# Packed attention and two feed-forwards on one core: a new instruction order for the second feed-forward

## The chip, the cores and the metric

The kernel runs on one core of a Trainium2 chip. The time is the device time of one execution in microseconds (us); a run of a kernel is one such execution, and the number compared is the median of several. The core has TensorE (PE in the rows, with its weight loads PEld), VectorE (DVE), ScalarE (ACT), GpSimd (POOL) and SyncE (SP), which issues the DMAs here. Each engine takes its instructions in the order in which the program lists them and waits on semaphores of the others.

## What is computed

Attention through 32 packed rows per head, then a gated feed-forward with RMS norm (width 512 to 1536), then a second feed-forward. Only the second one changes:

```python
def _moe2_ref(x, w_in, w_out):          # x: 4608 x 512, w_in: 512 x 2048, w_out: 2048 x 512
    h = x @ w_in
    g = h * np.cos(h)
    return (g @ w_out).astype(np.float32)
```

## The kernel before

All matrix products are made in three passes: each operand is split into a high and a low part (`hilo`, lines 110 to 112: a ScalarE copy, then a VectorE subtraction), and `mm3` (lines 154 to 157) multiplies high by high, high by low and low by high.

The second feed-forward is the loop from line 1107. The tokens come in nine chunks of 512 (`NCH`), the 2048 hidden columns in eight pairs of blocks of 128 (`NP2`); so there are 72 pairs `q`, and `p` is the pair before. For a pair, h is made by seven products of half-size blocks in place of eight (`prod(q, z, ...)`, six matmuls of 256 columns each), whose sums and differences are put together on VectorE and ScalarE: product 1 goes to PSUM tile `hx`, 2 to `hy`, 7 to `hz`, 6 adds to `hx`, 5 again to `hx`, 4 to `hz`, 3 to `hx`. Between them ScalarE copies intermediate states out: `p1` (line 1118, after product 1), `p7` (line 1128, after 7) and `u2` (line 1129, after 6); a later product on the same tile must wait until that copy has read it. VectorE adds `p1` (line 1121), `p7` (line 1144, into the second half of `hx`) and `u2` (line 1145). So h of a pair consists of two blocks, `s` = 0 (tile `h`, complete after product 4) and `s` = 1 (tile `hx`, complete after product 3 and line 1144).

For each block, g = h cos(h) is a chain of nine steps over 512 columns: `kk_a` (ScalarE, line 1026), `kk_b`, `r_a`, `r_b` (VectorE, 1030, 1034, 1040), `r_abs` and `r_sin` (ScalarE, 1044, 1048), `r_mul` (VectorE, 1052), `g_hi` (ScalarE, 1056) and `g_lo` (VectorE, 1060). In the trace the tiles are `kk`, `r` and `ghl`. Then `o_part` multiplies four token tiles of 128 by the block of the output weights (`w2hl`, split by `w2_split`), twelve matmuls of 512 columns for each block, into four PSUM tiles `ops` that collect all 16 blocks of a chunk. When a chunk is complete, `o_out` copies each tile to `ob` (ScalarE for even, VectorE for odd tiles, lines 1086 and 1084) and stores it (line 1098).

In the loop the second product of the pair two back, `o_part([(q - 2, 1)])`, stands in two stretches of two token tiles on either side of products 5 and 4, and `o_part([(q - 1, 0)])` behind product 3. While a chunk runs, the x of the next one is loaded and split on ScalarE and VectorE in pairs 2 to 7 of the chunk (`X_AT2`, `split_x`); `w_fetch(q + 3)` brings the first product's weights from DRAM, three buffers in all. The whole program has a fixed order (`tc.manual_schedule()`): every engine runs its instructions in the order of the code.

Of the kernel before, what the change touches and what calls it, by code (L numbers as in the profile page):

```python
# [9 lines left out]
F32 = mybir.dt.float32  # L10
F32R = mybir.dt.float32r
# [9 lines left out]
def kernel(  # L21
# [14 lines left out]
    nc = tc.nc  # L36
# [51 lines left out]
    X_AT = {11: (0,), 12: (1,), 13: (2,), 14: (3,), 15: (4,), 17: (5,), 19: (6,), 21: (7,)}  # L88
    X_AT2 = {2: (0,), 3: (1,), 4: (2,), 5: (3,), 6: (4, 5), 7: (6, 7)}
# [762 lines left out]
    def split_x(n, step):  # L852
        r0, r1 = x_r[n]
        lo, hi = slice(0, HT), slice(HT, TOK)
        a11, a21, a12, a22 = r0[:, :, lo], r0[:, :, hi], r1[:, :, lo], r1[:, :, hi]
        sub = lambda o, i0, i1: nc.vector.tensor_tensor(out=o, in0=i0, in1=i1, op=ALU.subtract)
        if step == 0:
            pool, tag = (late["b2"], "xs") if n else (pp_p, "pp0")
            x_s[0] = pool.tile([128, 2, HT], F32, tag=tag, name="xs", bufs=1)
            nc.vector.tensor_tensor(out=x_s[0], in0=a21, in1=a22, op=ALU.add)  # L860
            sub(a21, a11, a21)
            return
        src = (None, a11, a12, a21, a11, x_s[0], a12, a22)[step]
# [34 lines left out]
    def w2_load(f):  # L898
        assert ("o", f, 0) in w2_done
        pool, tag = late["w2"], ("raw", "ny")[f % 2]  # L900
        t = w2_r[f] = pool.tile([128, DM], F32, tag=tag, name="w2raw", bufs=2 + 2 * (f % 2))
        nc.sync.dma_start(out=t, in_=w2o_dram[f])
# [91 lines left out]
    for f in range(NF1):  # L994
        for d2 in range(2):
            acc_block(B, f, d2)
        if f + len(S_AT) < NF1:
            load_s(f + len(S_AT))
        w2_split(f)
        if f == NF1 // 2:  # L1000
            nc.scalar.activation(out=warm, in_=halfpi, func=AF.Sin)
        if f + 2 < NF1:
            w2_load(f + 2)
# [58 lines left out]
    def o_part(jobs, ts):  # L1062
        jobs = [j for j in jobs if j[0] >= 0]
        for t in ts:
            sl = slice(t * 128, (t + 1) * 128)
            for q, s in jobs:
# [6 lines left out]
                if k == NF2 - 1:  # L1073
                    o_out(n, t)
# [26 lines left out]
    def after(f, q, s):  # L1101
        if q >= 0:
            f(q, s)

    w_fetch(2)
    T = list(range(TOK // 128))
    for q in range(NQ + 1):
        p, on = q - 1, q < NQ
        n, fp = divmod(q, NP2)
        if on:  # L1110
            x = ps_h.tile([128, 2, HT], F32, tag="hx", name="hx", bufs=2)
            y, z = (ps_h.tile([128, 2, HT], F32, tag=t, name=t)[:, 0] for t in ("hy", "hz"))
            prod(q, 1, x[:, 0], True)
        after(r_mul, p, 0)
        after(r_abs, p, 1)
        if on:
            p1, p7, u2 = (b2.tile([128, HT], F32, tag=t, name=t, bufs=1) for t in ("p1", "p7", "u2"))
            nc.scalar.activation(out=p1, in_=x[:, 0], func=AF.Copy)
            prod(q, 2, y, True, True)
            h0 = b2.tile([128, 2, HT], F32, tag="h", name="h")  # L1120
            nc.vector.tensor_tensor(out=h0[:, 0], in0=y, in1=p1, op=ALU.add)
            prod(q, 7, z, True)
            prod(q, 6, x[:, 0], False)
        after(r_sin, p, 1)
        after(g_hi, p, 0)
        after(r_mul, p, 1)
        if on:
            nc.scalar.activation(out=p7, in_=z, func=AF.Copy)
            nc.scalar.activation(out=u2, in_=x[:, 0], func=AF.Copy)
        after(g_hi, p, 1)  # L1130
        after(g_lo, p, 0)
        if on:
            if n + 1 < NCH:
                if fp == 1:
                    load_x(n + 1)
                for step in X_AT2.get(fp, ()):
                    split_x(n + 1, step)
        after(g_lo, p, 1)
        if on:
            o_part([(q - 2, 1)], T[:2])  # L1140
            prod(q, 5, x[:, 0], False)
            prod(q, 4, z, False, True)
            o_part([(q - 2, 1)], T[2:])
            nc.vector.tensor_tensor(out=x[:, 1], in0=x[:, 0], in1=p7, op=ALU.add)
            nc.vector.tensor_tensor(out=h0[:, 1], in0=z, in1=u2, op=ALU.add)  # L1145
            h_t[q] = {"h": (h0.rearrange("p t n -> p (t n)"), x.rearrange("p t n -> p (t n)"))}
            kk_a(q, 0)
            kk_b(q, 0)
            r_a(q, 0)
            r_b(q, 0)  # L1150
            prod(q, 3, x[:, 0], False, True)
            w_fetch(q + 3)
            kk_a(q, 1)
            kk_b(q, 1)
            o_part([(q - 1, 0)], T)
            r_abs(q, 0)
            r_sin(q, 0)
            r_a(q, 1)
            r_b(q, 1)
        else:  # L1160
            o_part([(q - 2, 1)], T)
            o_part([(q - 1, 0), (q - 1, 1)], T)
# [30 lines left out]
```

## Time and profile before

| | us |
|---|---|
| median of three runs | 1658.41 |
| lowest and highest | 1651.59, 1667.56 |
| the profiled execution | 1651.87 |
| its span, first to last instruction | 1650.1 |
| TensorE busy | 1590.3 |
| VectorE, ScalarE busy | 1131.8, 897.1 |

The profiled execution is one of its own, beside the three. In it the second feed-forward's first product starts at 860.42 us and its last matmul at 1645.08 us. A matmul's busy time in the rows is longer than the distance between two starts, since matmuls overlap: 0.28 us for 256 columns at a distance of 0.12, 0.39 for 512 columns.

### The profile page before, as it was taken

The numbers are of one execution on the slowest core, as the hardware profiler recorded it, in microseconds if no ns is written. First come the engines' busy times: TensorE is split into PE (matmuls) and PEld (weight loads), VectorE is DVE, ScalarE is ACT, GpSimd is POOL, SyncE is SP. The second block draws the span as 40 slices with busy tenths as digits, with TensorE's granted clock in tenths as the row PEclk, the third lists the DMA queues.
The fourth block names the chain that finished last, engine by engine and source line by source line (L and its number), as shares of the span: only waits on it lengthen the run. The fifth ranks groups of instructions, "written<-read, shape, count | busy, mean of one in ns | idle before, by whom it ended". The sixth has DMA issues, their size and how long they took to land.

```text
span 1650.1 us, 29157 instructions
## 1 busy us (share of the span) xinstructions
PE 1590.3 (96%) x11216; PEld 1344.8 (82%) x11216; DVE 1131.8 (69%) x2203; ACT 897.1 (54%) x1796; POOL 32.8 (2%) x49
## 2 busy tenths in 40 slices
PE   7868999999999999999999999999999999999998
PEld 5536778888888787878988888888888888888887
DVE  4678866666666756665527777777777777777775
ACT  5556554455545454444426656565556565565654
POOL 1000110000000000000000000000000000000000
PEclk9989999999999999999999999999999999999999
DMA  9997644565555555556376454646454645454551
GB/s 265 310 257 236 200 149 148 168 190 165 184 186 172 178 182 180 196 163 207 104 276 227 179 209 165 220 179 230 169 201 174 228 179 214 171 209 179 183 200 26
DMA packets 129387, 315.97 MB, mean 191 GB/s; under 512 B 41696, under 2 KB 60128, under 8 KB 120032
## 3 DMA queue, kind: packets, MB, share of 16 engines
q1 hardware_dynamic: 129248, 314.10, 57.1%
q8 instruction: 89, 1.46, 0.4%
q14 instruction: 50, 0.41, 0.1%
HBM read 262.15 MB, written 51.90 MB: 190 GB/s over the span
## 4 chain that ended last, share of the span: by engine, by line
PE 87%; DMA 6%; DVE 3%; issue 1%; ACT 1%; POOL 0%; SPq 0%; DVEq 0%; POOLq 0%; ACTq 0%
PE ops L155 8%; PE ops L156 8%; PE ops L157 8%; PE gv L155 6%; PE acc L155 6%; PE gv L156 6%; PE gv L157 6%; PE acc L157 6%; PE acc L156 6%; PE hx L155 5%; PE hx L157 4%; PE hx L156 4%; PE mps L568 3%; DMA wo<-in_moe_w_gate_dram 2%; PE hz L155 2%; PE hz L156 2%
## 5 line engine op out<-in xcount | busy, mean ns | idle before, releaser
L155 PE MATMUL gv<-apt,wmhl 128*128 128x288 f32 x768 | 234.4, 305 | 1.7 <-ACT apt L111 0.9
L156 PE MATMUL gv<-apt,wmhl 128*128 128x288 f32 x768 | 228.3, 297 | 0.4 <-DVE apt L112 0.4
L156 PE MATMUL ops<-w2hl,ghl 128*128 128x512 f32 x576 | 227.1, 394 | 0.0
L155 PE MATMUL ops<-w2hl,ghl 128*128 128x512 f32 x576 | 227.0, 394 | 0.0
L157 PE MATMUL gv<-apt,wmhl 128*128 128x288 f32 x768 | 226.9, 295 | 0.0
L157 PE MATMUL ops<-w2hl,ghl 128*128 128x512 f32 x576 | 224.8, 390 | 0.0
L788 ACT ACTIVATE shl<-silu 128x288 fp32r<-128x288 f32 x192 | 85.4, 445 | 198.8 <-DVE silu L781 192.8
L155 PEld LDWEIGHTS gv<-apt,wmhl 128*128 128x128 f32 x768 | 145.4, 189 | 48.3 <-issue 17.3
L155 PE MATMUL acc<-shl,wohl 128*128 128x512 f32 x432 | 175.7, 407 | 1.2 <-ACT wohl L531 0.9
L157 PE MATMUL acc<-shl,wohl 128*128 128x512 f32 x432 | 170.2, 394 | 2.8 <-POOL wohl L534 2.7
L156 PE MATMUL acc<-shl,wohl 128*128 128x512 f32 x432 | 169.6, 393 | 0.0
L781 DVE TENSOR_TENSOR silu<-silu,gv 128x288 f32<-128x288 f32 x192 | 86.4, 450 | 99.9 <-PE gv L157 68.4
L156 PEld LDWEIGHTS gv<-apt,wmhl 128*128 128x128 f32 x768 | 145.2, 189 | 5.9 <-DVE apt L112 0.6
L157 PEld LDWEIGHTS gv<-apt,wmhl 128*128 128x128 f32 x768 | 145.2, 189 | 0.0
L1044 ACT ACTIVATE r<-r 128x512 f32<-128x512 f32 x144 | 91.1, 633 | 98.5 <-DVE r L1040 98.5
L1026 ACT ACTIVATE kk<-h,magic 128x512 f32<-128x512 f32 x72 | 52.1, 724 | 159.4 <-DVE h L1145 159.4
L157 PEld LDWEIGHTS ops<-w2hl,ghl 128*128 128x128 f32 x576 | 108.5, 188 | 24.7 <-DVE ghl L1060 0.5
L155 PEld LDWEIGHTS ops<-w2hl,ghl 128*128 128x128 f32 x576 | 109.1, 189 | 16.3
L156 PEld LDWEIGHTS ops<-w2hl,ghl 128*128 128x128 f32 x576 | 109.2, 190 | 14.9
L780 ACT ACTIVATE silu<-gv 128x288 f32<-128x288 f32 x192 | 78.4, 408 | 59.5 <-PE gv L157 58.7
L112 DVE TENSOR_TENSOR wmhl<-mps,wmhl 128x512 fp32r<-128x512 f32 x96 | 61.8, 685 | 70.5 <-ACT wmhl L111 70.5
L1060 DVE TENSOR_TENSOR ghl<-r,ghl 128x512 fp32r<-128x512 f32 x144 | 98.8, 686 | 11.9 <-ACT ghl L1056 11.8
(162 smaller groups left out, 3700.3 us busy)
## 6 DMA issues: line engine op xcount, KB each, us to landing
wa<-wa SPq DMA_DIRECT2D x72, 1024.0 KB, 4.9
wb<-wb SPq DMA_DIRECT2D x72, 768.0 KB, 6.5
wy<-wy SPq DMA_DIRECT2D x96, 512.0 KB, 4.6
kn<-in_k_dram SPq DMA_DIRECT2D x16, 576.0 KB, 9.5
vn<-in_v_dram SPq DMA_DIRECT2D x16, 576.0 KB, 9.2
qnat<-in_q_dram SPq DMA_DIRECT2D x32, 288.0 KB, 4.0
x_dram<-x SPq DMA_DIRECT2D x18, 512.0 KB, 3.1
x1raw<-x_dram SPq DMA_DIRECT2D x18, 512.0 KB, 8.1
```

The lines of the kernel that those rows point to most:

```text
L112: (eng or nc.vector).tensor_tensor(out=lo, in0=src, in1=hi.bitcast(F32), op=ALU.subtract)
L155: nc.tensor.matmul(ps, lhi, rhi, start=first, stop=False, skip_group_check=chain)
L156: nc.tensor.matmul(ps, lhi, rlo, start=False, stop=False, skip_group_check=chain)
L157: nc.tensor.matmul(ps, llo, rhi, start=False, stop=last, skip_group_check=chain)
L568: nc.tensor.matmul(ps[kt][h * NP:(h + 1) * NP], ppT[b // 4][rows, 4 * kt + h, n:n + NP], w_y[2 * u + kt][rows, j], start=True, stop=True,)
L780: nc.scalar.activation(out=t, in_=pss[0], func=AF.Silu)
L781: nc.vector.tensor_tensor(out=t, in0=t, in1=pss[1], op=ALU.mult)
L788: nc.scalar.activation(out=sh[:, 0, cols], in_=t, func=AF.Copy)
L1026: nc.scalar.activation(out=kk, in_=h, func=AF.Identity, scale=1.0 / TWO_PI, bias=magic[:, 0:1])
L1044: nc.scalar.activation(out=r, in_=r, func=AF.Abs)
L1060: nc.vector.tensor_tensor(out=g[:, 1], in0=h_t[q]["r", s], in1=g[:, 0].bitcast(F32), op=ALU.subtract)
```

## The change

Product 3 of a pair, which completes block `s` = 1, moves behind product 6 of the next pair (`p3`), and with it `kk_a`, `kk_b`, `r_a` and `r_b` of that block. The product of the pair two back stands in one stretch behind it, ahead of products 5 and 4; the other one ends the pair. The outputs of a chunk are no longer copied where they are complete, but collected (`outs`) and put at four places of the ScalarE and VectorE order (`o_evict`). `split_x` is divided into single steps: the high parts `h0` to `h6` and the sums `s1` to `s4`; `X_AT2` gives each pair two places, for ScalarE on either side of `p1` (`x_hi`), for VectorE behind `g_lo` of the pair before and between `kk_a` and `kk_b` (`x_lo`). The weights are fetched two pairs ahead, behind product 3 of the pair before. The splits of the output weights 10 and 11 move from the end of the first feed-forward into pairs 1 and 2, and their raw blocks lie in the two `pp` buffers. After the last pair the rest is written out, with one block's product after the other.

```diff
@@ -85,8 +85,10 @@
     AL_AT, CL_AT = 16, 21
     ATT_FROM, ATT_TO, ATT_FROM0, ATT_TO0, N_ATT = 0, 48, 10, 45, 32
     BX, BW = 9, 12
-    X_AT = {11: (0,), 12: (1,), 13: (2,), 14: (3,), 15: (4,), 17: (5,), 19: (6,), 21: (7,)}
-    X_AT2 = {2: (0,), 3: (1,), 4: (2,), 5: (3,), 6: (4, 5), 7: (6, 7)}
+    X_AT = {
+        11: ("s1", "s3"), 12: ("h0",), 13: ("h1", "s2"), 14: ("h2", "s4"), 15: ("h3",), 17: ("h4",), 19: ("h5",), 21: ("h6",)
+    }
+    X_AT2 = {2: ("s1", "s3"), 3: ("h0", "h1"), 4: ("s2", "h2"), 5: ("s4", "h3"), 6: ("h4", None), 7: ("h5", "h6")}
 
     wide = w_gate.dtype != F32
 
@@ -849,25 +851,31 @@
 
     x_r = {}
 
-    def split_x(n, step):
+    def split_x(n, step, part=None):
         r0, r1 = x_r[n]
         lo, hi = slice(0, HT), slice(HT, TOK)
         a11, a21, a12, a22 = r0[:, :, lo], r0[:, :, hi], r1[:, :, lo], r1[:, :, hi]
         sub = lambda o, i0, i1: nc.vector.tensor_tensor(out=o, in0=i0, in1=i1, op=ALU.subtract)
-        if step == 0:
-            pool, tag = (late["b2"], "xs") if n else (pp_p, "pp0")
-            x_s[0] = pool.tile([128, 2, HT], F32, tag=tag, name="xs", bufs=1)
-            nc.vector.tensor_tensor(out=x_s[0], in0=a21, in1=a22, op=ALU.add)
-            sub(a21, a11, a21)
+        if step[0] == "s":
+            if step == "s1":
+                pool, tag = (late["b2"], "xs") if n else (pp_p, "pp0")
+                x_s[0] = pool.tile([128, 2, HT], F32, tag=tag, name="xs", bufs=1)
+                nc.vector.tensor_tensor(out=x_s[0], in0=a21, in1=a22, op=ALU.add)
+            elif step == "s3":
+                sub(a21, a11, a21)
+            elif step == "s2":
+                sub(a11, x_s[0], a11)
+            else:
+                sub(a12, a12, a11)
             return
-        src = (None, a11, a12, a21, a11, x_s[0], a12, a22)[step]
-        t = wm_p.tile([128, 2, 2, HT], F32R, tag="wm", name="xhl")
-        x_t[n].append(t)
-        hilo(src, t[:, 0], t[:, 1])
-        if step == 2:
-            sub(a11, x_s[0], a11)
-        if step == 3:
-            sub(a12, a12, a11)
+        x = int(step[1])
+        src = (a11, a12, a21, a11, x_s[0], a12, a22)[x]
+        if part != 1:
+            x_t[n].append(wm_p.tile([128, 2, 2, HT], F32R, tag="wm", name="xhl"))
+            nc.scalar.activation(out=x_t[n][x][:, 0], in_=src, func=AF.Copy)
+        if part != 0:
+            t = x_t[n][x]
...
@@ -897,8 +905,11 @@
 
     def w2_load(f):
         assert ("o", f, 0) in w2_done
-        pool, tag = late["w2"], ("raw", "ny")[f % 2]
-        t = w2_r[f] = pool.tile([128, DM], F32, tag=tag, name="w2raw", bufs=2 + 2 * (f % 2))
+        if f in (NF1 - 2, NF1 - 1):
+            t = w2_r[f] = pp_p.tile([128, DM], F32, tag=f"pp{f % 2}", name="w2raw", bufs=1)
+        else:
+            tag = ("raw", "ny")[f % 2]
+            t = w2_r[f] = late["w2"].tile([128, DM], F32, tag=tag, name="w2raw", bufs=2 + 2 * (f % 2))
         nc.sync.dma_start(out=t, in_=w2o_dram[f])
...
@@ -996,7 +1007,8 @@
             acc_block(B, f, d2)
         if f + len(S_AT) < NF1:
             load_s(f + len(S_AT))
-        w2_split(f)
+        if f < NF1 - 2:
+            w2_split(f)
...
-    def o_part(jobs, ts):
+    def o_part(jobs, ts, outs=None):
...
@@ -1071,7 +1083,10 @@
                 k = o_n[n, t] = o_n.get((n, t), -1) + 1
                 mm3(o_t[n][t], g[:, 0, sl], g[:, 1, sl], w[:, 0], w[:, 1], k == 0, k == NF2 - 1)
                 if k == NF2 - 1:
-                    o_out(n, t)
+                    if outs is None:
+                        o_out(n, t)
+                    else:
+                        outs.append((n, t))
...
@@ -1102,64 +1117,102 @@
         if q >= 0:
             f(q, s)
 
+    def after(q, f, *a):
+        if q >= 0:
+            f(q, *a)
+
+    def x_hi(n, fp, slot):
+        if n + 1 < NCH and fp in X_AT2:
+            step = X_AT2[fp][slot]
+            if step is not None and step[0] == "h":
+                split_x(n + 1, step, 0)
+
+    def x_lo(n, fp, slot):
+        if n + 1 < NCH and fp in X_AT2:
+            step = X_AT2[fp][slot]
+            if step is not None:
+                split_x(n + 1, step, 1)
+
+    def o_evict(outs, n):
+        for x in outs[:n]:
+            o_out(*x)
+        del outs[:n]
+
     w_fetch(2)
     T = list(range(TOK // 128))
-    for q in range(NQ + 1):
-        p, on = q - 1, q < NQ
-        n, fp = divmod(q, NP2)
-        if on:
-            x = ps_h.tile([128, 2, HT], F32, tag="hx", name="hx", bufs=2)
-            y, z = (ps_h.tile([128, 2, HT], F32, tag=t, name=t)[:, 0] for t in ("hy", "hz"))
-            prod(q, 1, x[:, 0], True)
-        after(r_mul, p, 0)
-        after(r_abs, p, 1)
-        if on:
-            p1, p7, u2 = (b2.tile([128, HT], F32, tag=t, name=t, bufs=1) for t in ("p1", "p7", "u2"))
-            nc.scalar.activation(out=p1, in_=x[:, 0], func=AF.Copy)
-            prod(q, 2, y, True, True)
-            h0 = b2.tile([128, 2, HT], F32, tag="h", name="h")
-            nc.vector.tensor_tensor(out=h0[:, 0], in0=y, in1=p1, op=ALU.add)
-            prod(q, 7, z, True)
-            prod(q, 6, x[:, 0], False)
-        after(r_sin, p, 1)
-        after(g_hi, p, 0)
-        after(r_mul, p, 1)
-        if on:
-            nc.scalar.activation(out=p7, in_=z, func=AF.Copy)
-            nc.scalar.activation(out=u2, in_=x[:, 0], func=AF.Copy)
-        after(g_hi, p, 1)
-        after(g_lo, p, 0)
-        if on:
-            if n + 1 < NCH:
-                if fp == 1:
-                    load_x(n + 1)
-                for step in X_AT2.get(fp, ()):
-                    split_x(n + 1, step)
-        after(g_lo, p, 1)
-        if on:
-            o_part([(q - 2, 1)], T[:2])
-            prod(q, 5, x[:, 0], False)
-            prod(q, 4, z, False, True)
-            o_part([(q - 2, 1)], T[2:])
-            nc.vector.tensor_tensor(out=x[:, 1], in0=x[:, 0], in1=p7, op=ALU.add)
-            nc.vector.tensor_tensor(out=h0[:, 1], in0=z, in1=u2, op=ALU.add)
-            h_t[q] = {"h": (h0.rearrange("p t n -> p (t n)"), x.rearrange("p t n -> p (t n)"))}
-            kk_a(q, 0)
-            kk_b(q, 0)
-            r_a(q, 0)
-            r_b(q, 0)
-            prod(q, 3, x[:, 0], False, True)
-            w_fetch(q + 3)
-            kk_a(q, 1)
-            kk_b(q, 1)
-            o_part([(q - 1, 0)], T)
-            r_abs(q, 0)
-            r_sin(q, 0)
-            r_a(q, 1)
-            r_b(q, 1)
-        else:
-            o_part([(q - 2, 1)], T)
-            o_part([(q - 1, 0), (q - 1, 1)], T)
+    p3 = lambda q: prod(q, 3, h_t[q]["x"][:, 0], False, True)
+    for q in range(NQ):
+        p, n, fp = q - 1, q // NP2, q % NP2
+        if fp == 1 and n + 1 < NCH:
+            load_x(n + 1)
+        x = ps_h.tile([128, 2, HT], F32, tag="hx", name="hx", bufs=2)
+        y, z = (ps_h.tile([128, 2, HT], F32, tag=t, name=t)[:, 0] for t in ("hy", "hz"))
+        p1, p7, u2 = (b2.tile([128, HT], F32, tag=t, name=t, bufs=1) for t in ("p1", "p7", "u2"))
+        h0 = b2.tile([128, 2, HT], F32, tag="h", name="h")
+        h_t[q] = {"x": x, "h": (h0.rearrange("p t n -> p (t n)"), x.rearrange("p t n -> p (t n)"))}
+        prod(q, 1, x[:, 0], True)
+        prod(q, 2, y, True, True)
+        x_hi(n, fp, 0)
+        nc.scalar.activation(out=p1, in_=x[:, 0], func=AF.Copy)
+        nc.vector.tensor_tensor(out=h0[:, 0], in0=y, in1=p1, op=ALU.add)
+        x_hi(n, fp, 1)
+        after(p, r_abs, 0)
+        after(p, r_sin, 0)
+        prod(q, 7, z, True)
+        prod(q, 6, x[:, 0], False)
+        after(p, p3)
+        w_fetch(q + 2 if q else NCH * NP2)
+        outs = []
+        o_part([(q - 2, 1)], T, outs)
+        after(p, r_mul, 0)
+        after(p, kk_a, 1)
+        after(p, kk_b, 1)
+        after(p, r_a, 1)
+        after(p, r_b, 1)
+        after(p, g_hi, 0)
+        o_evict(outs, 2)
+        nc.scalar.activation(out=p7, in_=z, func=AF.Copy)
+        nc.scalar.activation(out=u2, in_=x[:, 0], func=AF.Copy)
+        o_evict(outs, 1)
+        after(p, g_lo, 0)
+        o_evict(outs, 1)
+        after(p, r_abs, 1)
+        after(p, r_sin, 1)
+        x_lo(n, fp, 0)
+        after(p, r_mul, 1)
+        after(p, g_hi, 1)
+        if q in (1, 2):
+            w2_split(NF1 - 3 + q)
+        prod(q, 5, x[:, 0], False)
+        prod(q, 4, z, False, True)
+        nc.vector.tensor_tensor(out=h0[:, 1], in0=z, in1=u2, op=ALU.add)
+        nc.vector.tensor_tensor(out=x[:, 1], in0=x[:, 0], in1=p7, op=ALU.add)
+        kk_a(q, 0)
+        x_lo(n, fp, 1)
+        kk_b(q, 0)
+        r_a(q, 0)
+        r_b(q, 0)
+        after(p, g_lo, 1)
+        o_part([(q - 1, 0)], T)
+    q = NQ - 1
+    p3(q)
+    o_part([(q - 1, 1)], T)
+    kk_a(q, 1)
+    r_abs(q, 0)
+    kk_b(q, 1)
+    r_a(q, 1)
+    r_b(q, 1)
+    r_sin(q, 0)
+    r_abs(q, 1)
+    r_mul(q, 0)
+    r_sin(q, 1)
+    g_hi(q, 0)
+    r_mul(q, 1)
+    g_lo(q, 0)
+    g_hi(q, 1)
+    g_lo(q, 1)
+    o_part([(q, 0)], T)
+    o_part([(q, 1)], T)
 
 
 # ---- launch: one core; inputs and outputs as the reference has them ----
```

ScalarE in a pair without splits or outputs, before. The names with numbers are tiles: `hx_10901` is this pair's `hx`, `r_10868` and `r_10898` are the two blocks of the pair before, `r_10975` is this pair's first block.

```order
L1118 ACTIVATE p1_10912<-hx_10901 128x256
L1048 ACTIVATE r_10898<-r_10898,halfpi_62 128x512
L1056 ACTIVATE ghl_10937<-r_10868 128x512
L1128 ACTIVATE p7_10913<-hz_10903 128x256
L1129 ACTIVATE u2_10914<-hx_10901 128x256
L1056 ACTIVATE ghl_10942<-r_10898 128x512
L1026 ACTIVATE kk_10972<-h_10922,magic_63 128x512
L1026 ACTIVATE kk_10988<-hx_10901,magic_63 128x512
L1044 ACTIVATE r_10975<-r_10975 128x512
L1048 ACTIVATE r_10975<-r_10975,halfpi_62 128x512
L1044 ACTIVATE r_11005<-r_11005 128x512
```

The same place with the change; here `hx_10883` is this pair's `hx` and `hx_10770` that of the pair before, `r_10867` and `r_10944` are the blocks of the pair before.

```order
L1156 ACTIVATE p1_10886<-hx_10883 128x256
L1056 ACTIVATE r_10867<-r_10867 128x512
L1060 ACTIVATE r_10867<-r_10867,halfpi_62 128x512
L1038 ACTIVATE kk_10941<-hx_10770,magic_63 128x512
L1068 ACTIVATE ghl_10947<-r_10867 128x512
L1174 ACTIVATE p7_10887<-hz_10885 128x256
L1175 ACTIVATE u2_10888<-hx_10883 128x256
L1056 ACTIVATE r_10944<-r_10944 128x512
L1060 ACTIVATE r_10944<-r_10944,halfpi_62 128x512
L1068 ACTIVATE ghl_10955<-r_10944 128x512
L1038 ACTIVATE kk_10971<-h_10889,magic_63 128x512
```

`kk` of the second block (`kk<-hx`) has moved from behind the first one's to the next pair, ahead of both copies `p7` and `u2`, and the first `ghl` with it; abs and sin of the second block now stand behind `u2`.

VectorE in the pair after a chunk's end, where the outputs are copied, before; `hx_10901` is `hx` of the pair before, `hx_11008` and `h_11029` are this pair's.

```order
L1052 TENSOR_TENSOR r_10975<-r_10975,h_10922 128x512
L1121 TENSOR_TENSOR h_11029<-hy_11009,p1_11019 128x256
L1052 TENSOR_TENSOR r_11005<-r_11005,hx_10901 128x512
L1060 TENSOR_TENSOR ghl_11044<-r_10975,ghl_11044 128x512
L1060 TENSOR_TENSOR ghl_11049<-r_11005,ghl_11049 128x512
L1084 COPY ob_11060<-ops_10213 128x512
L1084 COPY ob_11085<-ops_10215 128x512
L1144 TENSOR_TENSOR hx_11008<-hx_11008,p7_11020 128x256
L1145 TENSOR_TENSOR h_11029<-hz_11010,u2_11021 128x256
```

And with the change; `hx_10883` is `hx` of the pair before, `hx_10994` and `h_11000` are this pair's.

```order
L1157 TENSOR_TENSOR h_11000<-hy_10995,p1_10997 128x256
L1064 TENSOR_TENSOR r_10974<-r_10974,h_10889 128x512
L1042 TENSOR_SCALAR kk_11052<-kk_11052 128x512
L1046 SCALAR_TENSOR_TENSOR r_11055<-kk_11052,hx_10883 128x512
L1052 SCALAR_TENSOR_TENSOR r_11055<-kk_11052,r_11055 128x512
L1099 COPY ob_11060<-ops_10197 128x512
L1072 TENSOR_TENSOR ghl_11058<-r_10974,ghl_11058 128x512
L1099 COPY ob_11069<-ops_10199 128x512
L1064 TENSOR_TENSOR r_11055<-r_11055,hx_10883 128x512
L1188 TENSOR_TENSOR h_11000<-hz_10996,u2_10999 128x256
L1189 TENSOR_TENSOR hx_10994<-hx_10994,p7_10998 128x256
```

The two output copies stood directly ahead of the adds of `p7` and `u2`; now they stand on either side of the first `ghl` step, with the second block's multiplication between them and the adds, and the add of `u2` comes ahead of that of `p7`.

## Rows read from the trace of the kernel before

**Rows 1.** The page, busy us, share and instructions.

```profile
PE 1590.3 (96%) x11216; PEld 1344.8 (82%) x11216; DVE 1131.8 (69%) x2203; ACT 897.1 (54%) x1796; POOL 32.8 (2%) x49
```

**Rows 2.** Stretches between first hy products: us, busy (xinstructions) by engine, clock, DMA share, GB/s.

```profile
902.87:913.41 10.54, 10.54 (x68) 9.54 (x67) 7.73 (x15) 6.29 (x12) 0.00 (x0) 1.00 0.48 180
...
924.03:934.81 10.78, 10.78 (x68) 9.50 (x67) 8.41 (x16) 6.90 (x14) 0.00 (x0) 1.00 0.46 168
...
sum 76.04, PE 74.92 PEld 66.61 DVE 57.70 ACT 45.52 POOL 0.00; mean PE 10.70 PEld 9.52 DVE 8.24 ACT 6.50 POOL 0.00
...
881.79:1627.12 745.33, 736.34 (x4557) 656.96 (x4556) 560.71 (x1002) 446.92 (x832) 0.00 (x0) 1.00 0.52 188
```

**Rows 3.** Waits of PE from 860 us: total, times, longest.

```profile
PE hx L155 <- DVE hx L1144: 9.0, 8, 1.1
PE hx L155 <- ACT p L1118: 3.0, 1, 3.0
PE hx L155 <- ACT u L1129: 1.2, 2, 0.7
```

**Rows 4.** Timeline at an output pair, start and length first.

```profile
962.42 0.39 PE L157 MATMUL ops<-w2hl,ghl 128*128 128x512 f32 x1
962.85 0.69 DVE L1084 COPY ob<-ops 128x512 f32<-128x512 f32 x1 [1.98 <-PE ops L157]
963.46 0.42 DVE L1144 TENSOR_TENSOR hx<-hx,p 128x256 f32<-128x256 f32 x1
...
963.93 0.38 PE L155 MATMUL hx<-xhl,wa 128*128 128x256 f32 x1 [1.12 <-DVE hx L1144]
```

**Rows 5.** Timeline of PE in a pair that splits x.

```profile
925.35 0.28 PE L157 MATMUL hz<-xhl,wa 128*128 128x256 f32 x1
925.54 0.39 PE L155 MATMUL hx<-xhl,wb 128*128 128x256 f32 x1
925.76 0.28 PE L156 MATMUL hx<-xhl,wb 128*128 128x256 f32 x1
```

**Rows 6.** Timeline of an undisturbed pair, two places.

```profile
904.91 0.28 PE L157 MATMUL hx<-xhl,wb 128*128 128x256 f32 x1
...
905.23 0.39 ACT L1129 ACTIVATE u<-hx 128x256 f32<-128x256 f32 x1 [0.26 <-PE hx L157]
...
911.23 0.69 DVE L1040 SCALAR_TENSOR_TENSOR r<-kk,r 128x512 f32<-128x512 f32 x1
911.84 0.42 DVE L1030 TENSOR_SCALAR kk<-kk 128x512 f32<-128x512 f32 x1
```

**Rows 7.** Stretches around the first pairs.

```profile
860.42:881.79 21.37, 17.16 (x103) 15.69 (x102) 13.56 (x25) 11.18 (x21) 0.00 (x0) 0.84 0.89 322
874.01:877.42 3.41, 3.41 (x18) 3.41 (x18) 1.37 (x3) 0.66 (x1) 0.00 (x0) 0.50 0.87 336
855.00:860.42 5.42, 5.42 (x26) 4.49 (x24) 2.46 (x4) 1.86 (x3) 0.00 (x0) 1.00 0.00 0
```

**Rows 8.** Instruction groups, 882 to 1642 us: count, busy us, mean ns, idle before.

```profile
L1048 ACT ACTIVATE r<-r,halfpi 128x512 f32<-128x512 f32 x141 | 101.3, 719 | 2.3
...
L1040 DVE SCALAR_TENSOR_TENSOR r<-kk,r 128x512 f32<-128x512 f32 x140 | 96.9, 692 | 4.8
L1056 ACT ACTIVATE ghl<-r 128x512 fp32r<-128x512 f32 x142 | 88.8, 625 | 0.2 <-DVE r L1052 0.2
...
L1030 DVE TENSOR_SCALAR kk<-kk 128x512 f32<-128x512 f32 x140 | 59.3, 423 | 55.4 <-ACT kk L1026 55.4
...
L1026 ACT ACTIVATE kk<-hx,magic 128x512 f32<-128x512 f32 x70 | 48.4, 692 | 25.8 <-PE hx L157 24.6
```

**Rows 9.** Output stores on SP at the end, ns each.

```profile
L1098 SPq DMA_DIRECT2D out_dram<-ob x8: 466/532/602, 1642.0 to 1646.7; - x8
```

**Rows 10.** DMA issues from 882 us: KB, median us to landing.

```profile
wa<-wa SPq DMA_DIRECT2D x67, 1024.0 KB, 4.9
wb<-wb SPq DMA_DIRECT2D x67, 768.0 KB, 6.5
```

More of the change, by code (lines that the diff above doesn't have):

```diff
@@ L856, in split_x @@
         sub = lambda o, i0, i1: nc.vector.tensor_tensor(out=o, in0=i0, in1=i1, op=ALU.subtract)
-        if step == 0:
-            pool, tag = (late["b2"], "xs") if n else (pp_p, "pp0")
-            x_s[0] = pool.tile([128, 2, HT], F32, tag=tag, name="xs", bufs=1)
-            nc.vector.tensor_tensor(out=x_s[0], in0=a21, in1=a22, op=ALU.add)
-            sub(a21, a11, a21)
-            return
-        src = (None, a11, a12, a21, a11, x_s[0], a12, a22)[step]
-        t = wm_p.tile([128, 2, 2, HT], F32R, tag="wm", name="xhl")
-        x_t[n].append(t)
-        hilo(src, t[:, 0], t[:, 1])
-        if step == 2:
-            sub(a11, x_s[0], a11)
-        if step == 3:
-            sub(a12, a12, a11)
+        if step[0] == "s":
[9 more added lines that the diff above has]
+                sub(a12, a12, a11)
+            return
+        x = int(step[1])
[5 more added lines that the diff above has]
+            t = x_t[n][x]
+            nc.vector.tensor_tensor(out=t[:, 1], in0=src, in1=t[:, 0].bitcast(F32), op=ALU.subtract)
     x_s = [None]
```

## The prediction

> **What bounds the kernel now.** I read the page's busy shares first: TensorE is busy for 96% of the span, and VectorE and ScalarE for 69% and 54% [rows 1]. Its instructions are the same before and after, so the change can win or lose only time in which TensorE stands or runs slowly inside the second feed-forward, which lasts from 860.42 us to 1645.5 us. The second view cuts that stretch from one pair's first hy product to the next. An undisturbed pair takes 10.54 us: 42 products of 256 columns at 0.12 us from start to start and 24 of 512 columns at 0.228 us make 5.04 + 5.46 = 10.50 us, so TensorE never stands in it. But seven pairs around a chunk's end take 76.04 us in place of 7 x 10.54 = 73.78, that is 2.26 us too much; and the 69 whole pairs from 881.79 to 1627.12 us take 745.33 us, where 69 x 10.54 = 727.26. **So 18.1 us are lost there**, eight times the same pattern [rows 2]. The list of waits tells the largest part: eight waits of 1.12 us of hx on the add of line 1144 [rows 3]. The timeline shows why: line 1144 stands on VectorE behind the two output copies of line 1084. The second copy can start only when the fourth output tile is complete (last product at 962.42, copy at 962.85), and block product 3 waits for the add, so it begins 1.51 us after the last output product in place of 0.23 [rows 4]. The rest is small: in a pair that splits x for the next chunk, p1 on ScalarE stands behind the next-chunk copies and block product 6 starts 0.19 and 0.22 us apart in place of 0.12 [rows 5].
>
> The first two pairs have no second product to cover waits: 860.42 to 881.79 us is 21.37 us, with waits of 3.03 and 0.70 us [rows 3] and, after them, a granted clock of 0.50 (1.2 of 2.4 GHz), at which 18 products of 256 columns fill 3.41 us [rows 7].
>
> **The change, part by part.** Times are from a pair's first product, with durations from [rows 8]: the five VectorE steps over two 512-column blocks take 0.69 us each, line 1030 0.42, copies and abs on ScalarE 0.63, sin 0.72, kk 0.69; steps over 256 columns take 0.42 on VectorE [rows 4] and 0.39 on ScalarE [rows 6]. TensorE's new order is products 1, 2, 7, 6 and the previous pair's 3 (30 x 0.12 = 3.60), twelve products of the previous pair's second half-row (2.73, to 6.33), products 5 and 4 (to 7.77), twelve more (to 10.50).
>
> *Product 3 in the next pair.* The add of p7, now after product 4, ends at about 9.2; product 3 follows at 13.4. The waits on line 1144 go, and with them the pattern's largest term. What is late next has three deadlines.
> (a) Product 5 at 6.33 needs u2. ScalarE stands waiting for product 3; from its last product's start to a ScalarE start takes 0.32 us [rows 6], so kk begins at 3.80, ghl 0.6 later, p7 at 4.9, u2 at 5.2, done at 5.57: 0.7 us early.
> (b) The second stretch at 7.77 needs the low half of ghl of the previous pair's first half. Line 1030 follows kk at 4.53, then r in two steps to 6.40, then the subtraction, done at 7.0: 0.7 us early.
> (c) The other half's subtraction comes last on VectorE, at 12.3, and is wanted at 14.1.
> None of the three feeds on the wait of the pair before (p1 starts from product 1, kk from product 3), so nothing accumulates.
> In the split pairs one ScalarE copy lies ahead of p1, where the engine has been free since 9.8 of the pair before, and one behind it, which moves sin and the multiplication to about 4.1, still ahead of ghl at 4.4. The two subtractions lie on VectorE behind (b) and beside kk. I count them at nothing; if cover is gone they cost what they cost now, 0.1 to 0.2 us in four pairs of a chunk.
> In the output pairs one ScalarE copy precedes u2 (5.57 becomes 6.1 against 6.33) and one VectorE copy precedes (b)'s subtraction (7.0 becomes 7.6 against 7.77): still nothing, between 0 and 0.3 us each.
> **So I take the whole 18.1 us off**, with 3 us as the bound of what may stay.
>
> That sum lets independent VectorE instructions overlap: one of 0.69 us starts at 911.23 and the next at 911.84 [rows 6]. The Trainium skill ("VectorE: DVE Perf Modes", "The DRAIN you can't avoid") says that the next instruction starts only when the pipeline is empty. By that rule (b)'s subtraction in an output pair would come 0.1 us too late, 0.9 us over eight chunks, and the time would be 1644.5 us; the row speaks against it.
>
> *First pairs.* Product 3 of pair 0 moves behind product 6 of pair 1, but u2 of pair 1 still ends a serial chain: h, kk, 1030, r twice, abs, sin, multiply, ghl, p7, u2. From product 4's end at 5.0 (36 products and a wait of 0.6) that is 0.4 + 0.72 + 0.42 + 0.69 + 0.69 + 0.63 + 0.72 + 0.69 + 0.62 and two short steps, about 6.7 us, against 3.6 us of products: a wait of 3.2 us where 3.03 and 0.70 stand now. The next two pairs catch up with another 0.5 us each. I take 0.5 us of gain; the bounds are -2 and +2.6 (the half clock's share).
>
> *Late weight splits.* The w2 splits of blocks 10 and 11 leave the stretch before 860.42, where TensorE is busy for all of 5.42 us [rows 7], and go into pairs 1 and 2, before h of the second half. There is nothing to win before; behind, 0.6 us on VectorE at most, part of the catching up.
>
> *Weight fetch.* It is issued at 3.8 us of pair q for pair q+2, so 17 us ahead in place of 23; a fetch lands 4.9 and 6.5 us after its issues [rows 10]. On SP it stands behind the x loads and ahead of the output stores. Nothing.
>
> *The tail.* This part loses. In the last pair only product 3 (0.72 us) stands between the two stretches, so the stretch that (c) feeds is wanted at 11.2 and released at 12.4: **1.2 us**. It lasts to 15.1. The last pair's own chain then runs serially: r of the first half to 11.7, kk of the second at 11.4, r to 14.1, the first half's multiplication to 14.7, second sin to 15.5, ghl to 16.0, subtraction to 16.8: another **1.75 us**. Now the same place stands for some 0.2 us. That makes 2.8 us. The four output tiles also complete 0.68 us apart in place of 1.37, while SP needs two stores of 0.53 us for each [rows 9]; from the first copy's end, 1.25 us before TensorE's, eight stores end 3.1 us after it in place of 2.0 (SP's last issue now starts at 1646.7). **1.0 us.**
>
> *Sum.* 1651.87 - 18.1 - 0.5 + 2.8 + 1.0 = 1637.1 us for the profiled execution (1.8 us of it outside the span). That execution is the lower end of three, whose median is 1658.41; 14.8 us off the median give **1643.6 us**, 0.9% less. Differences under about 1% can hardly be told from none with this kernel's spread.
>
> **The rivals.**
> *The start runs at full clock.* The clock fell after a stall of 3.03 and one of 0.70 us close together [rows 3, 7]; one stall of 3.2 us may not bring it down. That returns up to 2.6 us: 1641. For it speaks that one stall replaces two; against it, that the long one stays.
> *The clock falls in the tail.* The two new stalls lie 2.7 us apart, with 24 products of 512 columns after the first. At half clock [rows 7] half of these would take 0.43 us in place of 0.228, so about 2.5 us more: 1646. The Trainium skill ("TensorE: Matmul & The Clock Gate", "Why this matters for your kernels") says that pauses between matmul bursts bring the half clock back; this trace agrees at 870 us, while no stall of its tail shows it.
> *The small waits stay.* p1 or the subtractions fall late in split and output pairs: 2.26 us per chunk shrink to about 0.9, so 7 us more: 1650.6.
> *ScalarE's order becomes the bound: slower than before.* u2 now stands behind kk, which waits for product 3, and behind ghl, which waits for VectorE's multiplication. If u2 comes d later than 6.33 in each of 70 pairs, that is 70 d; from d = 0.21 us the gain is gone, and at d = 0.4 the time is 1643.6 + 28 = 1672. For it: a wait in every pair, not in eight. Against it: the margin of 0.7 us, and VectorE's busy 8.4 us in a split pair of 10.78 [rows 2].
>
> **How the numbers follow.** The forecast has 0.55, the full clock at the start 0.15, the half clock in the tail 0.12, the small waits 0.13, slower 0.05. Faster by over 1% means below 1641.8: a third of the forecast's share (its terms are uncertain by 4 us), two thirds of the first rival's, a little of the second's, and the spread of the medians: 0.40. Slower by over 1%: 0.04. Within 1%: 0.56. The range leaves out the slower rival and the outermost tenth on the fast side: 1633 to 1654 us.
>
> **What would show it.** Right: pairs of 10.54 us throughout, no waits on the add of p7; one wait of about 3 us near 872 us on u2; two waits of 1.2 and 1.8 us in the last 25 us. Wrong: a wait of product 5 on u2, or of the second stretch on VectorE's subtraction, in the pairs between, or pairs whose length is not 10.54 us without a wait.

## The result and the profile after

The changed kernel takes **1643.38 us** in the median (1633.51 to 1648.39, 15 runs), the kernel before 1653.56 (1649.75 to 1667.56, 15 runs): the ratio is **0.9916**, 95% interval 0.9891 to 0.994. The interval lies below 1, so the gain is real, but it is about as small as this measurement can tell. The medians differ by 10.2 us. The profiled execution took 1636.35 us with a span of 1634.6, against 1650.1 before, which is 15.5 us less; that is the pair on which the prediction's sum was made, and 1637.1 was predicted.

The busy shares of the page hardly move, as [rows 1] let expect:

```profile
PE 1580.8 (97%) x11216; PEld 1343.2 (82%) x11216; DVE 1129.5 (69%) x2203; ACT 903.0 (55%) x1796; POOL 33.1 (2%) x49
```

The stretches say where the time went. First the kernel before, cut into first pairs, the 67 pairs from pair 4 on, last pair, and the end after TensorE (us, then busy us of TensorE, its weight loads, VectorE, ScalarE and GpSimd, then granted clock, DMA share, GB/s):

```profile
860.42:902.87 42.45, 38.24 (x235) 34.76 (x234) 29.39 (x54) 23.59 (x44) 0.00 (x0) 0.92 0.66 239
902.87:1627.12 724.25, 715.26 (x4425) 637.89 (x4424) 544.88 (x973) 434.51 (x809) 0.00 (x0) 1.00 0.52 189
1627.12:1645.31 18.19, 18.19 (x98) 15.23 (x96) 10.17 (x18) 9.41 (x17) 0.00 (x0) 1.00 0.11 23
1645.31:1650.10 4.79, 0.15 (x1) 0.00 (x0) 0.69 (x1) 0.00 (x0) 0.00 (x0) 0.72 0.62 133
```

The same stretches of the changed kernel, and within the second of them one pair that splits x and one that copies outputs, which answer to [rows 2]:

```profile
862.78:901.81 39.03, 35.25 (x229) 31.28 (x228) 26.74 (x50) 22.71 (x42) 0.00 (x0) 1.00 0.65 243
922.85:933.37 10.52, 10.52 (x68) 9.54 (x67) 7.80 (x15) 6.10 (x11) 0.00 (x0) 1.00 0.46 174
954.41:964.93 10.52, 10.52 (x68) 9.54 (x67) 8.09 (x15) 7.04 (x13) 0.00 (x0) 1.00 0.74 250
901.81:1606.65 704.84, 704.84 (x4424) 639.03 (x4423) 542.86 (x973) 440.71 (x807) 0.00 (x0) 1.00 0.53 195
1606.65:1628.10 21.45, 19.59 (x104) 15.88 (x102) 13.37 (x23) 11.61 (x20) 0.00 (x0) 1.00 0.01 2
1628.10:1634.60 6.50, 0.16 (x1) 0.00 (x0) 0.69 (x1) 0.11 (x1) 0.00 (x0) 0.70 0.74 158
```

All 67 pairs now take 10.52 us, those with outputs and with splits among them (67 x 10.52 = 704.84), so they gain 19.4 us. The first pairs gain 3.4; 0.72 of it is the product that comes later, so 2.7. The last pair takes 21.45 us, 0.72 of it that product, so it loses 2.5; the end loses 1.7. The stretch began 2.4 us later, at 862.78 in place of 860.42 us, though two weight splits had left the part ahead of it. That is spread between executions: with the same code ahead, it begins at 860.07, 859.85 and 858.88 us in e4, e5 and e6 below. -19.4 - 2.7 + 2.5 + 1.7 + 2.4 = -15.5 us, the difference of the spans.

The waits of TensorE from 855 us on, in place of [rows 3] (total, times, longest):

```profile
PE hx L157 <- ACT u L1175: 3.7, 3, 3.0
PE ops L157 <- ACT ghl L1068: 1.2, 1, 1.2
PE ops L159 <- DVE ghl L1072: 0.6, 1, 0.6
```

The eight waits on the add of p7 are gone, and no other came in their place before the last pair. What stands at an output pair now, in answer to [rows 4], from the timelines of ScalarE, VectorE and TensorE:

```profile
958.08 0.62 ACT L1068 ACTIVATE ghl<-r 128x512 fp32r<-128x512 f32 x1
958.60 0.59 ACT L1101 ACTIVATE ob<-ops 128x512 f32<-128x512 f32 x1
...
959.34 0.40 ACT L1175 ACTIVATE u<-hx 128x256 f32<-128x256 f32 x1
...
959.47 0.69 DVE L1052 SCALAR_TENSOR_TENSOR r<-kk,r 128x512 f32<-128x512 f32 x1
960.08 0.68 DVE L1099 COPY ob<-ops 128x512 f32<-128x512 f32 x1
960.68 0.68 DVE L1072 TENSOR_TENSOR ghl<-r,ghl 128x512 fp32r<-128x512 f32 x1
...
960.04 0.28 PE L157 MATMUL hx<-xhl,wb 128*128 128x256 f32 x1
...
961.47 0.40 PE L157 MATMUL ops<-w2hl,ghl 128*128 128x512 f32 x1
```

u2 ends at 959.74 and product 5 starts at 960.04: 0.30 us to spare behind one output copy. The subtraction of line 1072 ends at 961.36, behind another, and the second stretch starts at 961.47: 0.11 to spare. VectorE's instructions start 0.61 and 0.60 us apart here, though each is noted with 0.68 or 0.69. One after the other, from 959.47 on, the subtraction would have ended at 961.53, too late.

These starts agree with a section of the Trainium skill that the prediction did not weigh ("VectorE: DVE Perf Modes", "Two Vector instructions with no wait between them"): whether an instruction waits for the earlier ones to finish depends on the partitions at which its operands and theirs start, and here all start at the same. The rule of "The DRAIN you can't avoid" itself refers to that section for a next instruction that is not held; taken without it, the rule is not what these rows show.

The last pair and the end, from the timelines of TensorE, ScalarE and SP; with them belongs [rows 9]:

```profile
1617.40 0.40 PE L158 MATMUL ops<-w2hl,ghl 128*128 128x512 f32 x1
1618.40 0.50 PE L159 MATMUL ops<-w2hl,ghl 128*128 128x512 f32 x1 [0.60 <-DVE ghl L1072]
...
1620.60 0.40 PE L159 MATMUL ops<-w2hl,ghl 128*128 128x512 f32 x1
1622.19 0.50 PE L157 MATMUL ops<-w2hl,ghl 128*128 128x512 f32 x1 [1.19 <-ACT ghl L1068]
1622.52 0.40 PE L158 MATMUL ops<-w2hl,ghl 128*128 128x512 f32 x1
1622.99 0.50 PE L159 MATMUL ops<-w2hl,ghl 128*128 128x512 f32 x1
...
1626.88 4.95 SPq L1113 DMA_DIRECT2D out_dram<-ob  x8
```

Two waits, where two were predicted. They cost more than the 1.79 us that stands beside them: from 1617.40 to 1618.40 is 1.00 in place of 0.23, from 1620.60 to 1622.19 it is 1.59, and the products behind come late by another 0.1 to 0.24 us. The eight stores take 4.95 us and end 3.7 us after TensorE.

### The profile page after: what moved, and what is told of

Read it like the earlier page. It is cut to its first block, busy times and chain, and to the rows that moved or that the text cites. A ratio compares the mean times of both kernels' runs of the same rounds, so it can differ in the third digit from the quotient of the medians.

```text
span 1634.6 us, 29173 instructions
## 1 busy us (share of the span) xinstructions
PE 1580.8 (97%) x11216; PEld 1343.2 (82%) x11216; DVE 1129.5 (69%) x2203; ACT 903.0 (55%) x1796; POOL 33.1 (2%) x49
## 4 chain that ended last, share of the span: by engine, by line
PE 86%; DVE 5%; DMA 4%; ACT 3%; issue 2%; POOL 0%; SPq 0%; DVEq 0%; POOLq 0%; ACTq 0%
PE ops L157 8%; PE ops L158 8%; PE ops L159 8%; PE gv L157 6%; PE acc L157 6%; PE gv L158 6%; PE gv L159 6%; PE acc L159 6%; PE acc L158 5%; PE hx L159 4%; PE hx L157 4%; PE hx L158 4%; PE mps L570 3%; PE hz L159 2%; PE hz L157 2%; PE hz L158 2%
## 5 line engine op out<-in xcount | busy, mean ns | idle before, releaser
L1068 ACT ACTIVATE ghl<-r 128x512 fp32r<-128x512 f32 x144 | 90.5, 628 | 56.4 <-DVE r L1064 56.4
L1042 DVE TENSOR_SCALAR kk<-kk 128x512 f32<-128x512 f32 x144 | 61.5, 427 | 78.0 <-ACT kk L1038 76.0
```

The lines of the kernel that those rows point to most:

```text
L1042: nc.vector.tensor_scalar(out=kk, in0=kk, scalar1=-MAGIC, scalar2=None, op0=ALU.add)
L1068: nc.scalar.activation(out=g[:, 0], in_=h_t[q]["r", s], func=AF.Copy)
```

## The experiments

Two theories. **Product 3**, the prediction's: the pattern around a chunk's end goes because product 3 no longer follows the add of p7 within its pair. **Place**: it goes because output copies and split steps stand elsewhere in the orders of ScalarE and VectorE, and product 3 need not move for it. The first three kernels put the places into the kernel before, whose product 3 stays; the changed kernel ran beside them again. The last four are edits of the changed kernel.

**e1_copies.** The kernel before; the copy of the fourth output tile, on VectorE, comes behind the two adds.

```diff
...
-            o_part([(q - 2, 1)], T[2:])
+            outs = []
+            o_part([(q - 2, 1)], T[2:], outs)
+            if outs:
+                o_out(*outs[0])
             nc.vector.tensor_tensor(out=x[:, 1], in0=x[:, 0], in1=p7, op=ALU.add)
             nc.vector.tensor_tensor(out=h0[:, 1], in0=z, in1=u2, op=ALU.add)
+            if outs:
+                o_out(*outs[1])
```

> The kernel before with one edit: in the pair after a chunk's end, the last output copy on VectorE stands behind the adds of p7 and u2 in place of ahead of them; product 3 stays in its own pair. Theory 'place' (the wait came from where the copy stands, and product 3 need not move): the pair of 11.93 us becomes 10.5 to 10.6, the one behind it 10.54, and the second feed-forward is 11 to 12 us shorter than before; the split pairs keep 10.62 to 10.78. Theory 'product 3' (only its move frees the add): product 3 still waits for its add, the pair stays above 11.3 us and at most 5 us are gained.

Measured, stretches (a split pair, an output pair, the 67 pairs):

```profile
936.34:947.11 10.77, 10.77 (x68) 9.50 (x67) 8.41 (x16) 6.90 (x14) 0.00 (x0) 1.00 0.44 170
968.59:979.12 10.53, 10.53 (x68) 9.53 (x67) 7.63 (x15) 6.66 (x13) 0.00 (x0) 1.00 0.93 329
915.18:1626.92 711.74, 711.74 (x4424) 638.31 (x4423) 544.90 (x973) 433.56 (x809) 0.00 (x0) 1.00 0.52 192
```

and at the output pair, from the timeline:

```profile
973.09 0.42 DVE L1150 TENSOR_TENSOR hx<-hx,p 128x256 f32<-128x256 f32 x1
...
974.95 0.28 PE L155 MATMUL hx<-xhl,wa 128*128 128x256 f32 x1
...
975.15 0.69 DVE L1087 COPY ob<-ops 128x512 f32<-128x512 f32 x1 [0.96 <-PE ops L157]
```

The add is done at 973.51 and product 3 starts at 974.95, 0.22 us after the last output product; the copy comes behind both. The output pair falls from 11.93 to 10.53 us with product 3 where it was, the split pair keeps its 10.77, and the 67 pairs gain 12.5 us (11 to 12 were expected). The single time, 1651.66 us, tells nothing: ahead of the second feed-forward, where nothing was edited, this execution was 13.4 us later than that of before.

**e2_splits.** The kernel before with the changed kernel's single split steps: the next chunk's high parts stay behind g_hi on ScalarE, at most two a pair; on VectorE one step stands ahead of the pair's adds and one behind them, where all stood ahead before. The steps are also spread anew over the pairs (`X_AT2`).

```diff
...
-                for step in X_AT2.get(fp, ()):
-                    split_x(n + 1, step)
+                x_hi(n, fp, 0)
+                x_hi(n, fp, 1)
+                x_lo(n, fp, 0)
...
             kk_a(q, 0)
+            x_lo(n, fp, 1)
             kk_b(q, 0)
```

> The kernel before with the other part alone: the x of the next chunk is split in the change's single steps, two places a pair (high parts behind the second ghl on ScalarE, the rest ahead of the last ghl step and between kk and line 1030 on VectorE). Theory 'place': the pairs of 10.62, 10.78, 10.77 and the 10.70 behind them become 10.54, 5 to 6 us less than before; the output pair keeps 11.9. Theory 'product 3': the pairs stay as they are, within 0.1 us.

Measured (a split pair, the output pair, the 67 pairs), 1647.05 us:

```profile
924.84:935.38 10.54, 10.54 (x68) 9.54 (x67) 7.54 (x15) 6.42 (x13) 0.00 (x0) 1.00 0.46 175
956.46:968.39 11.93, 10.81 (x68) 9.46 (x67) 7.47 (x15) 6.69 (x13) 0.00 (x0) 1.00 0.91 326
903.76:1622.36 718.60, 709.62 (x4425) 638.89 (x4424) 544.74 (x972) 439.83 (x808) 0.00 (x0) 1.00 0.52 190
```

The split pairs are at 10.54, the output pair keeps its 11.93. The 67 pairs gain 5.65 us.

**e3_both.** Both edits in the kernel before.

> Both edits together in the kernel before: output copy behind the adds, x split in single steps; product 3, the two stretches of the second product and the tail stay as before. Theory 'place': all pairs from the fourth on take 10.54 us, 18 us less than before, and the tail has neither the two new waits (2.0 us) nor the late stores: 2 to 5 us faster than the change, a ratio to before of 0.987 to 0.991. Theory 'product 3': slower than the change by 5 us or more.

Measured: **1633.54 us** in the median (1632.9 to 1638.46, 6 runs), ratio **0.9877** (0.9851 to 0.9904). Stretches: an output pair, the 67 pairs, the last pair.

```profile
954.60:965.14 10.54, 10.54 (x69) 9.54 (x68) 7.64 (x15) 6.68 (x13) 0.00 (x0) 1.00 0.94 327
901.90:1608.16 706.26, 706.26 (x4424) 638.90 (x4423) 544.93 (x972) 439.27 (x808) 0.00 (x0) 1.00 0.53 194
1608.16:1626.33 18.17, 18.17 (x98) 15.24 (x96) 10.17 (x18) 9.42 (x17) 0.00 (x0) 1.00 0.11 23
```

18.0 us of the pairs' loss are gone (12.5 and 5.65 make 18.16) and the last pair takes its old 18.17. The move of product 3 is not needed for the gain.

**after_again.** The changed kernel once more, on the chip of the three above.

> The change itself once more, on the same chip as the kernel with both edits. Theory 'place': 2 to 5 us slower than that kernel, 14 to 18 us faster than before. Theory 'product 3': faster than that kernel. The first pairs: a stall of 3.0 us each time; whether the granted clock falls behind it may differ from run to run, 2 to 3 us.

Measured: 1635.63 us (1634.08 to 1645.39, 6 runs), ratio 0.9892 (0.9864 to 0.9921). From the stretch's start to the span's end its profile has 772.4 us, e3's 770.5; the two intervals overlap, so that e3 is the faster of the two is not shown by the times (2.1 us between the medians). First pairs and the 67 pairs:

```profile
862.11:901.70 39.59, 36.10 (x229) 32.84 (x228) 26.85 (x50) 22.83 (x42) 0.00 (x0) 0.96 0.64 240
901.70:1606.54 704.84, 704.84 (x4424) 639.06 (x4423) 543.01 (x973) 440.88 (x807) 0.00 (x0) 1.00 0.53 195
```

**e4_one_more, e5_two_more.** The changed kernel with one or two more ScalarE copies ahead of p7 in each pair from the second on (of r, into a tile that nobody reads): they take up u2's margin. The edit of e5, with two; e4 has `range(1)`:

```diff
         o_evict(outs, 2)
+        if p >= 0:
+            for _ in range(2):
+                nc.scalar.activation(out=b2.tile([128, TOK], F32, tag="dm", name="dm", bufs=1), in_=h_t[p]["r", 0], func=AF.Copy)
         nc.scalar.activation(out=p7, in_=z, func=AF.Copy)
```

> The change with one more ScalarE copy of 512 columns (0.63 us, its result unused) ahead of p7 and u2 in each pair but the first. With the margin of 0.7 us that the prediction gave u2: the ordinary pairs keep 10.52 us; the output pairs, where one copy stands there already, grow by 0.2 to 0.4; 2 to 4 us in all. Rival (the order is only just in time, each step added there is paid): each pair 0.5 us longer, 11.0 us, 36 us in all.

> The change with two more such copies there, 1.1 us of ScalarE. With the margin of 0.7 us: each pair grows by what is over it, 0.3 to 0.5 us, to 10.8 to 11.0, product 5 waiting for u2; the time is 25 to 35 us longer than the change's, slower than before. Rival (ScalarE has slack everywhere, it is busy for 55%): no pair grows by more than 0.1 us.

Measured: 1638.59 and 1678.73 us, beside 1660.03 for the kernel before on that chip (one run each). One more copy, which moves u2 by 0.52 us: a pair without outputs, an output pair, the 67 pairs.

```profile
900.49:911.03 10.54, 10.54 (x69) 9.55 (x68) 8.34 (x16) 7.03 (x13) 0.00 (x0) 1.00 0.46 174
953.16:964.05 10.89, 10.78 (x69) 9.46 (x68) 8.33 (x16) 7.48 (x14) 0.00 (x0) 1.00 0.74 248
900.49:1608.89 708.40, 707.54 (x4424) 638.69 (x4423) 543.40 (x972) 474.93 (x874) 0.00 (x0) 1.00 0.53 194
```

Two more, a pair without outputs and the 67 pairs, and where product 5 starts in another such pair, from the timeline:

```profile
912.76:923.83 11.07, 10.79 (x69) 9.46 (x67) 8.51 (x16) 8.06 (x15) 0.00 (x0) 1.00 0.45 167
901.70:1647.02 745.32, 722.45 (x4424) 633.65 (x4423) 548.17 (x972) 507.11 (x941) 0.00 (x0) 1.00 0.50 185
```

```profile
1007.18 0.39 PE L159 MATMUL ops<-w2hl,ghl 128*128 128x512 f32 x1
...
1007.42 0.37 ACT L1178 ACTIVATE u<-hx 128x256 f32<-128x256 f32 x1
...
1007.85 0.38 PE L157 MATMUL hx<-xhl,wb 128*128 128x256 f32 x1 [0.28 <-ACT u L1178]
1008.07 0.28 PE L158 MATMUL hx<-xhl,wb 128*128 128x256 f32 x1
```

In a pair without outputs of the changed kernel u2 ends 0.79 us ahead of product 5 (1001.33 and 1002.12). Two copies make u2 end 1.18 us later, so 0.39 should show; the pair grows by 0.55. The 67 pairs take 40.5 us more than the changed kernel's, where 25 to 35 were expected for the whole. The kernel is then slower than before: the rival in which ScalarE's order becomes the bound is a real mechanism, 0.79 us away in a pair without outputs. In the output pairs, with 0.30 us left, one copy is already too many (+0.37).

**e6_inline.** The changed kernel with the four output copies where the tiles are complete; product 3 stays in the next pair.

```diff
-        o_part([(q - 2, 1)], T, outs)
+        o_part([(q - 2, 1)], T)
```

> The change without its collected output copies: each tile is copied where its last product stands in the order, ahead of the previous pair's kk, line 1030 and ghl. Theory 'place': product 3's move doesn't help by itself; the output pair waits some 2.8 us for u2 and the subtraction, 13.3 us, 20 to 24 us more than the change, slower than before. Theory 'product 3': output pairs of 10.5 to 11 us, at most 4 us more.

Measured: 1667.84 us (one run). The output pair of the first chunk, that of the third, the 67 pairs:

```profile
952.19:967.15 14.96, 12.37 (x69) 10.63 (x67) 9.57 (x17) 7.29 (x13) 0.00 (x0) 0.89 0.68 231
1129.38:1142.75 13.37, 10.78 (x68) 9.45 (x67) 8.14 (x15) 7.29 (x13) 0.00 (x0) 1.00 0.74 252
899.59:1638.12 738.53, 717.80 (x4425) 647.57 (x4423) 544.65 (x973) 442.18 (x807) 0.00 (x0) 0.98 0.50 186
```

and in the first of these pairs, from the timeline:

```profile
958.01 0.69 DVE L1099 COPY ob<-ops 128x512 f32<-128x512 f32 x1 [0.67 <-PE ops L159]
958.62 0.68 DVE L1064 TENSOR_TENSOR r<-r,h 128x512 f32<-128x512 f32 x1
...
960.57 0.38 PE L157 MATMUL hx<-xhl,wb 128*128 128x256 f32 x1 [2.59 <-ACT u L1175]
```

The multiplication of line 1064, 2.02 us after the pair's first hy product in the changed kernel (956.43 against 954.41), stands behind the last copy and comes after 6.43; ghl, p7, u2 and product 5 follow it. In seven of the eight output pairs the granted clock stands at 0.50 for 3.4 us behind that wait; in the third it stays at 1.00. So the order itself costs 2.85 us an output pair (13.37 against 10.52; 13.3 was expected), 22.8 in all, where the kernel before pays 1.4 a pair; the clock makes it 33.7, more than the 20 to 24 expected. With the copies here, moving product 3 is not sufficient, and their place matters more than before. These are not the places of the kernel before, though: product 3 moved and the copies directly ahead of the adds was not run, so what the move would win by itself there is not shown.

**e7_early_w2.** The changed kernel with the weight splits of blocks 10 and 11 back in the first feed-forward.

```diff
...
-        if f < NF1 - 2:
-            w2_split(f)
+        w2_split(f)
...
-        if q in (1, 2):
-            w2_split(NF1 - 3 + q)
```

> The change with the output weights 10 and 11 split where they were before, at the end of the first feed-forward. If these splits make the third and fourth pair catch up (11.11 and 11.12 us): both become 10.52 and the start is 1.1 us shorter. Rival (the first pairs' chain does it): unchanged within 0.2 us.

Measured: 1633.84 us (one run), first pairs 39.40 us beside 39.59 of after_again, both with the half clock for 3.4 us:

```profile
859.88:899.28 39.40, 35.91 (x230) 32.81 (x228) 26.74 (x50) 21.87 (x41) 0.00 (x0) 0.96 0.64 241
```

In a start with 3.4 us of half clock the late splits cost some 0.2 us. The profile with 11.11 and 11.12 us in the third and fourth pair had no half clock there, so whether the splits lengthen those is not shown.

## Why the prediction was right, and where its reason was wrong

*What bounds the kernel, and the size of the loss.* Right: 18.1 us of the pairs' stretch were lost, and all of it went; 19.4 did, since each pair is also 0.02 us shorter than an undisturbed one of before (67 x 0.02 = 1.3). The starts show where: behind each switch from 256 to 512 columns the first six products of 512 columns start 0.229 to 0.235 us apart in place of 0.227, some 0.02 us in all, and a pair has two such switches now, three before. What was read wrong is the loss in the split pairs. ScalarE's copies for the next chunk are not what p1 waits behind:

```profile
924.58 0.63 ACT L1044 ACTIVATE r<-r 128x512 f32<-128x512 f32 x1 [0.47 <-DVE r L1040]
```

p1 starts behind this step at 925.12, and the step waits for VectorE, whose chain is late because two split steps stand ahead of its adds. In e2 only one stands ahead of the adds, ScalarE's copies stay behind g_hi, and the loss is gone.

*Product 3 in the next pair.* **This is the step that failed**, though its number held: it credited the largest part of the 18.1 us to the move of product 3 ("The waits on line 1144 go"), and looked at the new places of output copies and split steps only for what they may cost, not for what they win. e1 and e2 gain 12.5 and 5.65 us by the places alone, e3 gains 18.0 with both, and e6, with product 3 moved and the copies inline, needs 33.7 us more for the 67 pairs than the changed kernel, some 10.9 of it with the half clock. The prediction had read the cause itself in [rows 4], two copies ahead of the add on VectorE, and then took the edit that moves the waiter for the one that moves the wait. What the changed kernel has beyond these places (product 3's move and the orders, fetches and weight splits that come with it), from e3 and after_again: 1.4 us in 67 pairs and 1.0 in the first ones (41.34 against 39.59 + 0.72, both with 3.4 us at half clock) won, and 2.5 + 1.7 lost behind them. On balance it loses 1.8 us in these profiles.

*The margins.* (a) 0.79 us measured, 0.7 predicted; in output pairs 0.30 where 0.2 was worked out (6.1 against 6.33). (b) 0.70 in a pair without outputs (1002.85 to 1003.55) and 0.11 in an output pair where 0.17 stood. The sum of overlapping VectorE instructions was right to some hundredths of a microsecond.

*First pairs.* One stall of 3.0 us, predicted 3.2; the two pairs behind it catch up with 0.6 each (11.1 us in place of 10.52), predicted 0.5. The gain was 2.7 us where 0.5 was taken, just beyond the bound of 2.6: 1.0 is the order, the rest goes with the granted clock (0.92 over that stretch before, 0.96 in e3 and after_again, 1.00 here). That rival (the start at full clock) came true in the profiled execution, whose granted clock there is 1.00, and not in after_again (0.96), where the clock fell behind one such stall.

*Weight splits and weight fetch.* 0.2 us for the splits in e7's start, within the 0.6 allowed; no wait on a fetch stands in the list of waits.

*The tail.* 2.5 us, predicted 2.8. The first wait was 0.9 with the late products, not 1.2: the stretch starts with two products of the high half, and only the third wants line 1072's output. The second was 1.7, predicted 1.75. The granted clock stayed 1.00 through both, so that rival did not happen here. It is real all the same: in e5 the clock stood at 0.50 for 3.4 us behind a wait of 1.5 us in the tail, and the last pair took 23.22 us.

*The end.* Mis-sized: 1.0 predicted, 1.7 measured. Eight stores were counted at 0.53 us, 4.24; queued without a pause they took 4.95.

*From the sum to the median.* 1637.1 predicted and 1636.35 measured for the profiled execution is nearer than the terms are: the pairs gave 1.3 us more than forecast, the first pairs 2.2 and the last pair 0.3, while the end took 0.7 more and the later start, which is spread, 2.4. That 1643.6 met 1643.38 is in good part luck: 14.8 us were taken off a median of 1658.41, while the medians of 15 runs are 1653.56 and 1643.38, 10.2 us apart; in the other set of runs they are 1652.82 and 1635.63, 17.2 apart.

## What to carry to other kernels

When an engine waits on one late instruction, look at what stands ahead of that instruction in its engine's order before moving the work that waits for it: here one copy put behind two adds, and split steps put behind them too, did what a rewritten pipeline did, without a longer tail. A reordered pipeline is as good as its smallest margin in its fullest iteration (0.11 us in the output pairs, where 0.70 stood in the others), so work the margins out there. Whatever is deferred by one iteration is paid once at the end of the loop; price that tail (4.2 us here) against what each iteration gains (0.02 us).

## What was not expected of the hardware

The granted clock in the first pairs differs between executions of the same instructions: the changed kernel had no half clock there in one profile and 3.4 us of it in the next (1.00 and 0.96 over the stretch), with a stall of 3.0 us in both. That is 0.56 us between the two first stretches (39.03 and 39.59), more than the 0.2 of the late weight splits. Of the ten profiles one has no half clock there, seven have 3.4 us, and two, of the kernel before and of e6, 6.8. And in e6 the same wait of 2.59 us, eight times, was followed by 3.4 us of half clock seven times.

A wait costs more than the list of waits says. TensorE's wait of 0.28 us in e5 made the pair 0.55 us longer: the product starts 0.44 us late by the pace of starts (1007.18 + 0.23 against 1007.85), since the list counts from the modelled end of the product before, and the one behind it follows after 0.22 in place of 0.12. The eight waits of 1.12 us of [rows 3] cost 1.39 each, and the two of the tail, 1.79 together, cost 2.5.

Single times mislead at this size: e1 gains 12.5 us where it was edited, and its one time is 1.2 us below the median of the kernel before, because its execution lost 13.4 us ahead of that place.
